# Laying out the inputs by their loads, regrouping on 128 partitions, and two early 128-row blocks in a Fourier-mixing and expert kernel

## The chip, the cores and the metric

The kernel runs on one core of a Trainium2 chip. The core has TensorE (PE, matrix products; its weight loads are shown as PEld), VectorE (DVE), ScalarE (ACT), GpSimd (POOL) and SyncE (SP), which run their own instruction streams and wait for each other through semaphores, and 16 DMA engines that move data between the on-chip memory SBUF and the device memory. SP, ACT and POOL issue DMAs. The metric is the time of one execution on the device, in microseconds; less is better.

## The reference, cut to what matters

Two layers follow each other. The first takes the real part of a two-dimensional Fourier transform of each batch, the second sends each row to one of eight experts, chosen by the largest gate value.

```python
x: (8, 2496, 256)                       # 8 batches, 2496 rows, 256 columns
X = np.fft.fft(np.fft.fft(x, axis=1), axis=2).real
x = X.reshape(19968, 256)
logits = x @ w_gate                      # (19968, 8)
e = argmax(logits); gate_w = softmax(logits)[e]
h = np.maximum(x @ w1[e], 0.0)           # w1[e]: (256, 1024)
y = gate_w * (h @ w2[e])                 # w2[e]: (1024, 256)
```

The weights of one expert are 2 MB in float32.

## The kernel before

All loops are unrolled in Python, and the order in which the instructions are written is the order in which each engine and each queue runs them (`manual_schedule`). Waits are put in by the framework where data or buffers need them.

*The transform.* The 2496 rows of a batch are taken as 104 x 24: row `24 n + j` lies on partition `n` at place `j`. `first(b)` computes the transform along the 104, in `NQ = 3` chunks `q` of four places `j`. Because the input is real, place `j` is combined with its mirror: `load_x` (L269) loads four near places by SP into `xl`, and gathers the mirrored rows by an indirect DMA of POOL, in reversed order, into `xh`; place 0 comes by its own load, `x0`. `fold` (L286) adds the mirror to the near rows on DVE, with reversed columns, and `fold_d` folds the columns; `half1` (L297) multiplies with the wave constants `w1` on PE, and ACT copies out. Then SP stores the result to the device memory, `Td[b]` (L337), and `load(b + 1, q - 1)` loads the next batch into the freed buffers. In three chunks `first` yields 12 times.

`regroup(b, h)` (L347) reads `Td[b]` back in another order, 120 rows on 120 partitions, in two halves of 6 and 5 groups (`t4`). `second(b)` (L357) does the transform along the 24 (`group`), then along the columns together with the gate (`p3`), in two halves `h` of `HW = 5` tiles of 128; each tile gives 2 x 128 rows, the second being mirrored. After each half `route` (L412) finds each row's expert and its place among the expert's rows, and POOL scatters the rows to the array `Xs` in device memory, ordered by expert: ten indirect DMAs (`put_row`, L212) of 128 rows in each half, twenty a batch. `second` yields after each step: 3 times before the first half, then in each half five times for its tiles, three times in `route` and ten times for the scatters.

*The experts.* The rows are worked on in blocks of one expert. `rounds()` (L131) says how many blocks of which size are certain to be there after each batch: after batch 0 two of 256 rows and four of 128, after batch 1 four of 256, then blocks of 512, and at the end 5 of 512, 7 of 256 and 21 of 128 for the rest. `plan` (L463) computes on DVE, from the counters of the experts, a table of each block's first row and expert, which SP reads into registers. `fetch` (L507) issues on SP the block's rows (`xb`, L512) and the two weight matrices (`w_sb`, L515 and L517). `experts` (L533) turns the rows on PE (`pt`), computes the hidden layer (`ph`, evicted with the maximum by ACT and DVE in turn), the second product (`py`), scales it on ACT and scatters 128 rows at a time to the output with POOL (L586). Weights have three buffers; up to three blocks are fetched ahead. 163 row tiles of 128 are computed for 156 of data, since a block has one expert.

*The order.* At the start come constants, the loads of batch 0 and 12 warm-up matmuls. Then `first(0)`, `regroup(0, ...)`, and `second(0)` with the steps of `first(1)` between. Then `experts` runs through the blocks of all rounds, and with it, in steps spread over 70% of each round's work (`TICKS`), the next batch's `second` and the transform `first` of the one after. `sent` and `taken` (L217) tell the framework which scatters a block's rows do not depend on: those of the following round.

Of the kernel before, what the change touches and what calls it, by code (L numbers as in the profile page):

```python
# [130 lines left out]
def rounds():  # L131

    want = [((256, 2), (128, 4)), ((256, 4),)] + [((512, B),)] * (B - 2)
    plan, used = [], 0

    def full(done, size):
        return max(0, -(-(done - used - E * (size - 1)) // size))

    for b in range(B):
        done = (b + 1) * S
        now = []
        for size, most in want[b]:
            k = min(full(done, size), most)
            if k:
                now.append((size, k, False))
            used += size * k
        if b == B - 1:
            k = full(done, BLK)  # L150
            used += BLK * k
            now.append((BLK, k, False))
            now.append((REST, (NT - used + E * (REST - 1)) // REST, True))
        plan.append(now)
    return plan


def in_order():

    todo = []  # L160
    for b, now in enumerate(rounds()):
        parts = [[(b, size, last, i) for i in range(k)] for size, k, last in now]
        if b == B - 1:
            few, many = parts[-2:]
            n = len(many) // len(few)
            rest = [x for i, y in enumerate(few) for x in [y] + many[n * i:n * (i + 1)]] + many[n * len(few):]
            parts = parts[:-2] + [rest]
        todo += sum(parts, [])
    return todo


TICKS = 44
WARM = 12
MOST = max(k for now in rounds() for _, k, _ in now)


# [15 lines left out]
def kernel(ctx: ExitStack, tc, x, w_gate, w1, w2, out):  # L192
# [28 lines left out]
    def taken(ins, b):  # L221
        ins = getattr(ins, "ins", ins)
        if b + 1 < B:
            tc.declare_no_dep(ins, group=f"xs{b + 1}", reason="a block has rows of its round's batches alone")
        tc.add_to_no_dep_group("taken", ins)
# [10 lines left out]

    ix = cp.tile([NA, B, NQ], I32, name="ix")
    pool.iota(ix[:], [[S // 4, B], [-1, NQ]], base=NB // 4 * NA - 1, channel_multiplier=-(NB // 4))
    pad = cp.tile([128, W], F32, name="pad")
# [23 lines left out]
    waves = const_dram("w1", consts["w1"])  # L263


    xall = x.rearrange("b (p j) d -> (b p) j d", j=NB)
    xrows = x.rearrange("b (n j) d -> (b n) (j d)", j=4)

    def load_x(b, q):  # L269
        xl = xp.tile([NP, 4, D], F32, tag="xl", name="xl", bufs=3)  # L270
        xh = xp.tile([NA, 4, D], F32, tag="xh", name="xh", bufs=3)
        n = NP if b + 1 < B else NA
        nc.sync.dma_start(out=xl[0:n], in_=xall[NA * b:NA * b + n, 4 * q + 1:4 * q + 5])
        pool.indirect_dma_start(  # L274
            out=xh[:].rearrange("p j d -> p (j d)"), out_offset=None, in_=xrows,
            in_offset=bass.IndirectOffsetOnAxis(ap=ix[:, b, q:q + 1], axis=0))
        return xl[0:NA], xh[:]

# [6 lines left out]

    def fold(xl, xh, q):  # L286

        n = 3 if q == NQ - 1 else 4
        a, m = xl, xh
        vec.tensor_tensor(free(a, 1, [D, n], [1, D - 1]), free(a, 1, [D, n], [1, D - 1]),  # L290
                          free(m, 3 * D + D - 1, [-D, n], [-1, D - 1]), op=ALU.add)
        yield
        vec.tensor_tensor(free(a, 0, [D, n]), free(a, 0, [D, n]), free(m, 3 * D, [-D, n]), op=ALU.add)
        fold_d(m, a, 4)
        yield
# [14 lines left out]

    def load(b, q):
        if b < B:
            ahead[b, q] = load_x(b, q)
        if b < B and q == 0:
            n = NP if b + 1 < B else NA
            x0 = xp.tile([NP, D], F32, tag="x0", name="x0")
            nc.sync.dma_start(out=x0[0:n], in_=xall[NA * b:NA * b + n, 0])
            ahead[b, "x0"] = x0[0:NA]

    def first(b):  # L320

        pm0 = xp.tile([NA, D], F32, tag="pm0", name="pm0")
        for q in range(NQ + 1):
            f = iter(())
            if q < NQ:
                xl, xh = ahead.pop((b, q))
                f = fold(xl, xh, q)
            next(f, None)
# [6 lines left out]
            if q:  # L335
                half1(b, q - 1, 1, pm, pm0, t1)
                nc.sync.dma_start(out=Td[b][:, 4 * (q - 1) * D:4 * q * D], in_=t1[:].rearrange("p j d -> p (j d)"))  # L337
                load(b + 1, q - 1)
            next(f, None)
            if q == 1:  # L340
                fold_d(pm0[:], ahead.pop((b, "x0")), 1)
            pm = xh
            yield
# [3 lines left out]
    def regroup(b, h):  # L347
        t4 = sp.tile([GP, HALF, D], F32, tag="t4", name="t4")
        n = min(HALF, NG - h * HALF)
        nc.sync.dma_start(  # L350
            out=t4[:, 0:n], in_=bass.AP(Td[b].tensor, Td[b].offset + h * HALF * GP * D,
                                        [[D, GP], [GP * D, n], [1, D]]))
        ahead[b, "t4", h] = t4
# [3 lines left out]
    def second(b):  # L357
# [3 lines left out]
        def turn_last(h):  # L361
# [4 lines left out]
            pr = pm_.tile([GP, HALF], F32, tag="m", name="pr")  # L366
            mm(pr[:, 0:n], con["rot"][:], t4[:, 0:n, H])
            act.copy(t4[:, 0:n, H], pr[:, 0:n])

        def group(g):  # L370
            i, n = g % HALF, LAST if g == NG - 1 else GP
            p2 = pm_.tile([128, 2, n], F32, tag="m", name="p2")
            for c in range(2):
                mm(p2[:, c], t4[:, i, c * H:(c + 1) * H], con["m2"][:, c, 0:n])
            act.copy(zz[:, :, g * GP:g * GP + n], p2[:])  # L375
# [36 lines left out]
    def route(b, h, rows, lg):  # L412
# [40 lines left out]
        for s in range(NSL):  # L453
            sent(put_row(Xs, pi[:, s:s + 1], rows[:, s], E * CAP - 1, "xs"), b)
            yield
# [50 lines left out]

    def fetch(b, size, tab, i):  # L507
        n = size // 128
        row = nc.sync.value_load(tab[:, 0, i:i + 1], min_val=0, max_val=ROWS - size)
        ev = nc.sync.value_load(tab[:, 1, i:i + 1], min_val=0, max_val=E - 1)  # L510
        xb = bp.tile([128, BIG // 128, W], F32, tag="xb", name="xb", bufs=3)
        taken(nc.sync.dma_start(out=xb[:, 0:n].rearrange("p t c -> p (t c)"),  # L512
                                in_=Xs[ds(row, size)].rearrange("(p t) c -> p (t c)", t=n)), b)
        w1_sb = bp.tile([128, 2, F], F32, tag="w1", name="w1_sb", bufs=3)
        nc.sync.dma_start(out=w1_sb[:], in_=w1[ds(ev, 1)].rearrange("o (c p) f -> p (o c) f", p=128))  # L515
        w2_sb = bp.tile([128, FC, D], F32, tag="w2", name="w2_sb", bufs=3)
        nc.sync.dma_start(out=w2_sb[:], in_=w2[ds(ev, 1)].rearrange("o (c p) d -> p (o c) d", p=128))  # L517
        return xb, w1_sb, w2_sb

# [13 lines left out]
    def experts(todo):  # L533
# [5 lines left out]
        def fetch_some(k, most=3):  # L539

            while k + len(got) < len(todo) and len(got) < most and todo[k + len(got)][:3] in tabs:
                b, size, last, at = todo[k + len(got)]
                got.append(fetch(b, size, tabs[b, size, last], at))

        for k, (b, size, last, at) in enumerate(todo):
            n, m = size // 128, BIG // size
            if not k:
                while todo[0][:3] not in tabs:
                    yield 0
                fetch_some(0)  # L550
                for _ in range(9):
                    yield 0
# [38 lines left out]
    def pads(b):  # L591
# [3 lines left out]
        for e in range(E):  # L595
            sent(put_row(Xs, ti[:, e:e + 1], pad[:], ROWS - 1, "xs"), b)
            yield
# [10 lines left out]
    def close(b):  # L608

        for size, k, last in rounds()[b]:  # L610
            yield from plan(b, size, k, last)

# [20 lines left out]
    load(0, 0)  # L633
    act.dma_start(out=con["w1"][:, 4:], in_=waves[:, 4:])
    for _ in range(WARM):
        pw = psy.tile([128, D], F32, tag="y", name="py")
        mm(pw[:], ones[:], bc(ones[:], 1, 2))
    load(0, 1)
    load(0, 2)
    act.dma_start(out=con["rt"][:], in_=const_dram("rt", consts["rt"]))  # L640
    act.dma_start(out=wg[:], in_=w_gate.rearrange("(c p) e -> p c e", p=128))
    nc.sync.dma_start(out=table[:], in_=const_dram("table", packed))
    nc.sync.dma_start(out=bt[:], in_=const_dram("blocks", cv))
    sent(unordered(nc.sync.dma_start(
        out=Xs[E * CAP:].rearrange("(k p) w -> p k w", k=BLK // 128), in_=bc(pad[:], 1, BLK // 128)), "xs"), 0)
    warm = cp.tile([1, 1], F32, name="warm")
# [5 lines left out]
    for _ in first(0):  # L652
        pass
    regroup(0, 0)
    regroup(0, 1)
    vec.tensor_copy(tri[:], con["tri"][:])
    for c in range(2):
# [7 lines left out]
        else:  # L665
            vec.tensor_copy(con["rd"][:, c, to + E:to + 2 * E], pg[:])
    early = ahead_of(1)
    for _ in range(7):
        next(early)
    for k, _ in enumerate(second(0)):  # L670
        if k % 2 == 0:
            next(early, None)
    work = experts(todo)
    for b in range(1, B):

        side, done, due = mixed(b), 0, 0.0
        if b == 1:
            side = woven(close(0), chain(early, side))
        total = 16 * sum(k * size for size, k, _ in rounds()[b - 1]) / BIG
        while done < total:  # L680
# [15 lines left out]


# [18 lines left out]
```

## Time and profile before

The median of 17 executions is 1412.75 us (1408.42 to 1416.7). The profiled execution took 1411.51 us, its span is 1409.7.

| engine | busy us | share of the span | instructions |
|---|---|---|---|
| PE | 1337.8 | 95% | 6186 |
| PEld | 1016.8 | 72% | 6186 |
| DVE | 382.5 | 27% | 1206 |
| POOL | 350.0 | 25% | 360 |
| ACT | 283.2 | 20% | 656 |

In 1409.7 us the DMA engines move 248.81 MB, 176 GB/s. All matmuls but a few are in float32. In the tables below a row names line, engine, operation and tiles as out<-in; `w_sb` stands for both weight tiles, `s`, `p` and `t` for the tiles of the two transform stages, `xT` for the turned rows. A busy time of PE is that of a pipeline and does not say at which clock it ran; the granted clock stands beside it as a share of full speed. "issue" is time in which an engine waited for nothing that the profile shows, "another core or an unknown queue" a wait whose releaser has no record.

### The profile page before, as it was taken

How to read it: one execution, taken by the hardware profiler on the slowest of the kernel's cores; microseconds unless marked ns; L12 is line 12 of the kernel's file. 1: busy time of each engine (PE TensorE's matmuls, PEld its weight loads, DVE VectorE, ACT ScalarE, POOL GpSimd, SP SyncE). 2: the span in 40 equal slices, each digit the busy share in tenths (PEclk: the TensorE clock that was granted, in tenths of full speed). 3: DMA queues.
4: the chain of work that ended last, by engine and by line, in shares of the span. 5: the costliest groups of instructions: out<-in, count | busy, mean ns of one | idle time of the engine just before them, and what ended most of it. 6: DMA issues, size and time to landing. Idle time of an engine off the chain costs nothing.

```text
span 1409.7 us, 17245 instructions
## 1 busy us (share of the span) xinstructions
PE 1337.8 (95%) x6186; PEld 1016.8 (72%) x6186; DVE 382.5 (27%) x1206; ACT 283.2 (20%) x656; POOL 350.0 (25%) x360
## 2 busy tenths in 40 slices
PE   4667898999999999999999999999999999999998
PEld 3556787776677667777677667776667679999997
DVE  3553243333341223332142221233211111111111
ACT  1322132132132111321132211221111111111111
POOL 1343314333214311324113311323311111111111
PEclk9758999999999999999999999999999999999999
DMA  8858877744645442562434442334422348888883
GB/s 233 221 195 262 264 233 236 258 128 121 242 128 176 141 168 94 182 189 100 166 101 138 141 167 94 113 112 143 167 105 97 92 140 272 273 266 267 267 270 99
DMA packets 134517, 248.81 MB, mean 176 GB/s; under 512 B 11245, under 2 KB 93839, under 8 KB 134432
## 3 DMA queue, kind: packets, MB, share of 16 engines
q1 hardware_dynamic: 114438, 194.38, 43.1%
q0 software_dynamic: 19344, 52.37, 10.8%
q10 hardware_dynamic: 650, 0.97, 0.3%
q8 instruction: 49, 0.80, 0.2%
q14 instruction: 36, 0.29, 0.1%
HBM read 194.28 MB, written 54.83 MB: 177 GB/s over the span
## 4 chain that ended last, share of the span: by engine, by line
PE 57%; issue 30%; POOL 6%; DMA 3%; another core or an unknown queue 1%; ACT 1%; DVE 1%; POOLq 0%; SPq 0%; ACTq 0%; DVEq 0%
PE py L197 23%; PE ph L197 23%; PE p L197 6%; POOL out_dram L212 4%; PE s L197 3%; PE pt L528 2%; POOL Xs L212 1%; DMA xh<-in_x_dram,ix 1%; DMA t<-Td 1%; DMA Td<-t 1%; DMA w_sb<-in_moe_w_dram 0%; PE rk L197 0%; POOLq L212 0%; DMA xb<-Xs 0%
## 5 line engine op out<-in xcount | busy, mean ns | idle before, releaser
L197 PE MATMUL ph<-xT,w_sb 128*128 128x512 f32 (+2 forms) x2112 | 589.0, 433 | 4.3 <-ACT hT L572 2.4
L197 PE MATMUL py<-w_sb,hT 128*128 128x256 f32 x2608 | 584.3, 380 | 6.2 <-issue 6.0
L197 PEld LDWEIGHTS py<-w_sb,hT 128*128 128x128 f32 x2608 | 489.4, 191 | 69.7 <-issue 7.0
L197 PEld LDWEIGHTS ph<-xT,w_sb 128*128 128x128 f32 x2112 | 341.8, 192 | 200.0 <-issue 177.1
L212 POOL DMA_INDIRECT out_dram<-y,ro x163 | 158.8, 975 | 849.8 <-ACT y L585 822.0
L570 DVE TENSOR_SCALAR hT<-ph 128x512 f32<-128x512 f32 x163 | 112.7, 692 | 704.9 <-issue 361.6
L585 ACT ACTIVATE y<-py,xb 128x256 f32<-128x256 f32 x163 | 77.1, 473 | 621.0 <-PE py L197 554.0
L212 POOL DMA_INDIRECT Xs<-rows,pi x160 | 158.4, 990 | 126.7 <-issue 78.7
L572 ACT ACTIVATE hT<-ph 128x512 f32<-128x512 f32 x163 | 97.3, 597 | 318.7 <-PE ph L197 297.7
L529 DVE TENSOR_SCALAR xT<-pt,table 128x512 f32<-128x512 f32 (+1 forms) x94 | 63.4, 674 | 64.5 <-PE pt L528 62.9
L197 PE MATMUL s<-xh,w 104*112 104x256 f32 (+2 forms) x208 | 61.9, 423 | 18.6 <-DVE xh L284 16.3
L197 PEld LDWEIGHTS p<-table,t 120*128 120x128 f32 x352 | 56.5, 210 | 28.1 <-issue 13.4
L404 DVE COPY lg<-p 128x16 f32<-128x16 f32 x80 | 14.0, 175 | 209.4 <-ACT zs L401 142.9
L197 PE MATMUL p<-table,zz 128*128 128x145 f32 (+1 forms) x320 | 59.6, 313 | 11.4 <-issue 5.4
L197 PE MATMUL p<-table,t 120*128 120x120 f32 (+1 forms) x352 | 59.5, 296 | 9.6 <-ACT hT L572 4.5
L197 PEld LDWEIGHTS s<-xh,w 104*112 104x112 f32 x208 | 39.6, 204 | 31.7 <-DVE xh L284 14.6
L197 PEld LDWEIGHTS p<-table,zz 128*128 128x128 f32 x320 | 48.3, 205 | 15.7 <-issue 8.2
L528 PEld LDWEIGHTS pt<-table,xb 128*128 128x128 f32 x326 | 40.7, 142 | 16.8 <-issue 11.6
L528 PE MATMUL pt<-table,xb 128*128 128x128 f32 x326 | 51.8, 275 | 0.9 <-DMA xb<-Xs 0.9
L406 DVE SCALAR_TENSOR_TENSOR rows<-p,zs 128x129 f32<-128x129 f32 x160 | 48.4, 344 | 1.6 <-issue 0.4
L274 POOL DMA_INDIRECT xh<-in_x_dram,ix x24 | 24.6, 1024 | 76.3 <-PE s L197 48.9
L375 ACT COPY zz<-p 128x240 f32<-128x240 f32 (+1 forms) x88 | 31.0, 352 | 52.2 <-PE p L197 37.0
(84 smaller groups left out, 333.2 us busy)
## 6 DMA issues: line engine op xcount, KB each, us to landing
w_sb<-in_moe_w_dram SPq DMA_DIRECT2D x132, 1024.0 KB
xb<-Xs SPq DMA_DIRECT2D x28, 516.0 KB
Td<-t SPq DMA_DIRECT2D x24, 448.0 KB
xl<-in_x_dram SPq DMA_DIRECT2D x21, 448.0 KB
t<-Td SPq DMA_DIRECT2D x8, 720.0 KB
t<-Td SPq DMA_DIRECT2D x8, 600.0 KB
xb<-Xs SPq DMA_DIRECT2D x13, 258.0 KB
xb<-Xs SPq DMA_DIRECT2D x25, 129.0 KB
```

The source lines that it names most:

```text
L197: nc.tensor.matmul(o, lhsT=lhsT, rhs=rhs, start=start, stop=stop, **kw)
L212: return unordered(pool.indirect_dma_start(out=dst, out_offset=bass.IndirectOffsetOnAxis(ap=idx, axis=0), in_=rows, in_offset=None, bounds ...
L274: pool.indirect_dma_start(out=xh[:].rearrange("p j d -> p (j d)"), out_offset=None, in_=xrows, in_offset=bass.IndirectOffsetOnAxis(ap=ix[: ...
L375: act.copy(zz[:, :, g * GP:g * GP + n], p2[:])
L404: vec.tensor_copy(lg[:, k:k + 2], p3[:, NY:NY + 2 * E].rearrange("p (m e) -> p m e", m=2))
L406: vec.scalar_tensor_tensor(rows[:, k + m, 0:NY], p3[:, 0:NY], zs[:, 0:1], zs[:, 1:], op0=ALU.add, op1=op)
L528: nc.tensor.transpose(pt[:, c, t], xb[:, 2 * h + t, c * 128:(c + 1) * 128], ident[:])
L529: vec.tensor_scalar(xT[:, :, 256 * h:256 * h + 128 * n], pt[:].rearrange("p c t k -> p c (t k)"), con["alt"][:], None, op0=ALU.mult)
L570: vec.tensor_scalar(o, ph[:], 0.0, None, op0=ALU.max)
L572: act.activation(o, ph[:], ACTF.Relu)
L585: act.activation(y[:, i], py[:], ACTF.Copy, scale=xb[:, i, D + 1:D + 2])
```

## The change

The inputs are laid out anew before the launch, in `laid`: `x` becomes one array in which the 104 partitions' eight places of a load (four near ones and their mirrors, already reversed; place 0 fills a gap of the third) follow each other, 8 KB a partition; the weights become 8 KB a partition in the order of their tiles. So a chunk is one plain load by SP; the gathers of POOL, the index list `ix` and the load of place 0 are gone. `regroup` reads 128 partitions, of which 120 are used. The stores `Td` of batches 0 and 1 are issued by ACT. The loads of batch 1 come after `first(0)`, two ahead of the regroup and one behind it; those of batch 2 are issued together, after the regroup of batch 1.

There is a new first round: two blocks of 128 rows that are certain to be there after the first half of batch 0 is routed; the round after batch 0 has one block of 256 less. The tables for it are computed at steps 11 to 15 of `second(0)` (`AFTER = 10`), the weights of its first block, the regroup of batch 1, the first block's rows and the loads of batch 2 are issued at step 20, in that order, and the steps of `first(1)` go to the places in `FILL`. `fetch` is split in weights and rows. The blocks' independence now covers two following rounds.

```diff
-    want = [((256, 2), (128, 4)), ((256, 4),)] + [((512, B),)] * (B - 2)
+    want = [((128, 2),), ((256, 1), (128, 4)), ((256, 4),)] + [((512, B),)] * (B - 2)
-    for b in range(B):
-        done = (b + 1) * S
+    for b in range(B + 1):
+        done = b * S if b else 2 * 128 * HW - NB
...
-WARM = 12
+WARM = 16
+FILL = (-1,-1,-1,3,5,7,11,11,11,12,13,14)
+ZERO = 3
+AFTER = 5 + HW
...
-    def load_x(b, q):
...
+    def load(b, q):
+        if b < B:
+            xq = xp.tile([NP, 8, D], F32, tag="xq", name="xq", bufs=3)
+            row = (b * NQ + q) * NA
+            nc.sync.dma_start(out=xq[:].rearrange("p j d -> p (j d)"), in_=x[row:row + NP])
+            ahead[b, q] = xq[0:NA]
...
-    def fold(xl, xh, q):
...
+    def fold(xq, q, pm0):
+        a, m = xq[:, 0:4], xq[:, 4:8]
+        n = 4
+        if q == NQ - 1:
+            n = 3
+            fold_d(pm0, m[:, 3], 1)
+        vec.tensor_tensor(a[:, 0:n], a[:, 0:n], m[:, 0:n], op=ALU.add)
+        yield
         fold_d(m, a, 4)
...
-                nc.sync.dma_start(out=Td[b][:, 4 * (q - 1) * D:4 * q * D], in_=t1[:].rearrange("p j d -> p (j d)"))
-                load(b + 1, q - 1)
+                (nc.sync if b > 1 else act).dma_start(out=Td[b][:, 4 * (q - 1) * D:4 * q * D], in_=t1[:].rearrange("p j d -> p (j d)"))
+                if b > 1:
+                    load(b + 1, q - 1)
...
-        t4 = sp.tile([GP, HALF, D], F32, tag="t4", name="t4")
+        t4 = sp.tile([128, HALF, D], F32, tag="t4", name="t4")
...
-            sent(put_row(Xs, pi[:, s:s + 1], rows[:, s], E * CAP - 1, "xs"), b)
+            sent(put_row(Xs, pi[:, s:s + 1], rows[:, s], E * CAP - 1, "xs"), b + 1 if b or h else 0)
...
     def fetch(b, size, tab, i):
...
+        nc.sync.dma_start(out=w1_sb[:], in_=w1[ds(ev, 1)].rearrange("o p c f -> p (o c) f"))
...
+    def fetch_rows(b, size, tab, i):
...
             if not k:
                 while todo[0][:3] not in tabs:
                     yield 0
+                w = fetch(b, size, tabs[b, size, last], at)
+                yield 0
+                got.append((fetch_rows(b, size, tabs[b, size, last], at), *w))
+                yield 0
                 fetch_some(0)
-                for _ in range(9):
+                for _ in range(ZERO):
                     yield 0
...
     load(0, 0)
-    act.dma_start(out=con["w1"][:, 4:], in_=waves[:, 4:])
+    load(0, 1)
+    nc.sync.dma_start(out=con["w1"][:, 4:], in_=waves[:, 4:])
+    load(0, 2)
+    nc.sync.dma_start(out=table[:], in_=const_dram("table", packed))
+    nc.sync.dma_start(out=con["rt"][:], in_=const_dram("rt", consts["rt"]))
+    nc.sync.dma_start(out=wg[:], in_=w_gate)
...
     for _ in first(0):
         pass
+    load(1, 0)
+    load(1, 1)
     regroup(0, 0)
     regroup(0, 1)
+    load(1, 2)
...
-    early = ahead_of(1)
-    for _ in range(7):
-        next(early)
+    early = first(1)
+    work = experts(todo)
+    for _ in range(FILL.count(-1)):
+        next(early, None)
+    first_blocks = plan(0, *rounds()[0][0])
     for k, _ in enumerate(second(0)):
-        if k % 2 == 0:
+        for _ in range(FILL.count(k)):
             next(early, None)
-    work = experts(todo)
+        if k > AFTER:
+            next(first_blocks, None)
+        if k == AFTER + 4:
+            next(work)
+        if k == AFTER + 2 * HW:
+            for _ in early:
+                pass
+            next(work)
+            regroup(1, 0)
+            regroup(1, 1)
+            next(work)
+            for q in range(NQ):
+                load(2, q)
...
+def laid(x, moe_w_gate, moe_w1, moe_w2):
+    n1, i = np.arange(NA)[:, None], np.arange(4)[None]
+    back = -np.arange(D) % D
+    thirds = []
+    for q in range(NQ):
+        s = NB * n1 + 4 * q + 1 + i
+        far = x[:, -s % S][..., back]
+        if q == NQ - 1:
+            far[:, :, 3] = x[:, ::NB]
+        thirds.append(np.concatenate([x[:, s], far], 2))
+    xs = np.stack(thirds, 1).reshape(-1, 8 * D)
...
```

## The prediction

> **What bounds the kernel now.** I read the engine table first, then the tables by stage, the chain of waits and the DMA table. By stage (times in us; busy time and instructions of PE, PEld, DVE, ACT, POOL; granted clock, DMA share, GB/s):
>
> ```profile
> 0.00:43.00 43.00, 18.46 (x58) 12.19 (x58) 17.12 (x45) 6.17 (x10) 7.83 (x12) 0.86 0.87 226
> 43.00:97.00 54.00, 36.45 (x188) 30.35 (x188) 29.46 (x131) 18.14 (x56) 24.65 (x23) 0.66 0.65 192
> 97.00:195.00 98.00, 83.82 (x468) 74.82 (x469) 29.21 (x105) 18.29 (x45) 29.34 (x30) 0.88 0.89 284
> 400.00:1409.00 1009.00, 1004.04 (x4579) 752.55 (x4577) 233.17 (x680) 190.52 (x419) 222.92 (x229) 1.00 0.49 162
> ```
>
> From 400 us on TensorE is busy 1004.04 of 1009 us: nothing there can be won except by giving it less work, and the work stays (163 row tiles of 128). What can be won lies before 400, most of it before 97, when the first expert block starts: until then PE has two transform stages of batch 0 and part of batch 1, small work at a granted clock of 0.66 to 0.86. The chain of waits names what it waits for (start, length, what):
>
> ```profile
> 3.23 15.24 DMA xh<-in_x_dram,ix
> 29.10 7.56 DMA Td<-t
> 36.68 6.32 DMA t<-Td
> 71.03 3.40 another core or an unknown queue
> 87.31 2.34 DMA Xs<-rows,pi
> 90.56 6.45 DMA w_sb<-in_moe_w_dram
> 97.14 3.75 PE ph L197 x8
> 102.72 1.75 PE ph L197 x8
> 122.42 3.01 another core or an unknown queue
> 125.81 3.81 another core or an unknown queue
> 154.80 6.04 issue
> 220.52 8.57 another core or an unknown queue
> 321.84 2.25 issue
> ```
>
> In order: gathered inputs, the store and reload of the transposed batch 0, then (between 60.85 and 88.28, twenty lines of one kind) the scatters of batch 0, and only then the expert weights. The first group of eight hidden-layer matmuls takes 3.75 us, the second 1.75: the first ran on a slow clock. Six pieces with no named releaser sum to 27.1 us. The scatters, from the timeline of POOL, first and last:
>
> ```profile
> 60.85 1.02 POOL L212 DMA_INDIRECT Xs<-rows,pi  x1 [2.79 <-DVE rows L406]
> 87.31 0.97 POOL L212 DMA_INDIRECT Xs<-rows,pi  x1 [0.30 <-issue]
> ```
>
> Each takes 1.0 plus 0.3 us; twenty take 27.4. Last, two DMA rates: the first 45 us, and the best weight loading (270 to 275 us):
>
> ```profile
> DMA packets 4732, 10.26 MB, mean 228 GB/s; under 512 B 805, under 2 KB 2668, under 8 KB 4732
> DMA packets 976, 1.95 MB, mean 391 GB/s; under 512 B 47, under 2 KB 654, under 8 KB 975
> ```
>
> **The change part by part.**
>
> *Inputs.* Now the fold waits for gathers that share the engines with everything issued at the start: the first fold starts at 14.67, the third load's at 21.51, and the last store of batch 0 issues at 29.10, 7.59 after that. The change makes one queue of it in order of need. Up to and with the third load there are 3 x 917 KB of inputs, 186 and 513 KB of wave constants: 3.45 MB. At 228 GB/s that is 15.1 us, at 391 it is 8.8; the first packets move at 1.6 and I give 1.5 for the last to be seen. I take 300 GB/s, between the ends because the rows are now 8 KB in sequence, like the weights, but the first 45 us are the nearest in place: 11.5 + 3.1 = 14.6 (ends 11.9 and 18.2). The three folds before it take 2.76 each (1.22, 0.69, 0.68, 0.17 in the timeline) and do not bind. With the fold of column 0 now ahead of the third add (0.7) the last store issues at 14.6 + 0.7 + 7.6 = 22.9 (20.2 to 26.5).
>
> *Store and regroup.* The store took 7.56 behind 0.9 MB of next-batch loads. It goes to ACT's queue; by 22.9 the issued bytes are 3.45 + 0.77 (tables) + 1.83 (two loads of batch 1, put ahead of the regroup) + 1.38 (stores) = 7.43 MB, 24.8 us at 300 GB/s, so it lands at 28 (ends: 3 us at the fast rate, 7.56 as before). The regroup took 6.32; now 786 KB over 128 partitions at the 235 GB/s of 40 to 45 us, 3.3 + 2 = 5.3 (4.5 to 6.3). Batch 0 can go on at 33.3 instead of 43.0; ends 27.7 and 40.4. *A rule against this:* the Trainium skill (DMA: Bandwidth & Descriptors, "Issuing engines are not separate DMA queues") says that issuing from another engine saves issue time alone, since all queues share the same DMA engines. By it the store would take 7.56 again and the end would be 2.5 us later, inside my slow end; the row cannot tell, as it has one queue only.
>
> *Issue cost.* Six stores on ACT cost 0.3 to 0.6 us of its queue each (its four issues at the start take 0.61, 0.31, 0.38, 0.75); three lie among batch 0's copies, at most 1.5 us on the chain, kept below. Twenty-four gathers of 1.02 + 0.3 us leave POOL; it is 25% busy, and the scatters of batch 0 have none between them, so I take 0. One add instead of two saves DVE 0.16 x 24, hidden: DVE is 27% busy. Four more warm matmuls (0.2 us each) end before the first input. Weights in 8 KB rows: in 145 to 150 us, when 1 KB rows of w2 moved, 278 GB/s; best 391. Where PE is full this is worth 0; in 97 to 195 at most 1 us a block; I take 0.
>
> *Batch 0's second stage.* From its first matmul (43.13) to the first scatter (60.85) are 17.7 us, with 5.1 us of batch 1's matmuls between. Now two of their halves are left there (2 x 0.86 to 1.7): 16 us with ACT's issues. First scatter at 49.5, ten at 62.5, twenty at 76, landed 2.34 later: 64.8 and 78.3, against 89.65 now.
>
> *The two early blocks.* Their rows are fetched at 65. SP has been past the weights of block 0 by then (2.1 MB, no longer after the rows, which saves the 6.45 of the chain), but the two regroups of batch 1 (1.41 MB, 6 us at 235 GB/s) stand ahead in its queue, and they wait for batch 1's stores and for batch 0's last group; three loads of batch 2 stand behind. Rows land near 72. A 128-row block takes 7.25 us at full clock (spacing of the last blocks, 1382.40 to 1389.65), up to twice that on a slow one: 73 to 84. Block 1's weights come last of what is issued from 50 on: 2.1 + 0.9 (stores) + 1.4 + 0.1 + 2.75 + 2.2 + 2.6 (twenty scatters of 132 KB) = 12.1 MB. At 340 GB/s (317 in 90 to 130 us, 363 in 120 to 125) 36 us: 86. Block 1 runs 86 to 94, and the next block of 256 rows, whose rows were there at 78.3 and whose 2.4 MB need 7 us more, starts at 94, not at 97.1 as the first block of 256 does now. *A rule against it:* the Trainium skill (TensorE: Matmul & The Clock Gate, "Why this matters for your kernels") says an idle gap beyond some 3 us puts the array back to half clock. The 3.75 against 1.75 us agree; by it block 0 costs 14.5 instead of 7.25, which my 73 to 84 has room for since block 1 waits for its weights anyway.
>
> *Sum.* 97.1 - 94 = 3.1 earlier, two row tiles of 7.15 already done = 14.3, the cold first group no longer at the head of the long run = 2.0: 19.4. One 256-row block becomes two of 128: 2 x 7.25 - 14.3 = +0.2 and 2 MB more weights, early. The stage 97 to 195 did 8 tiles (57) and 15 of transform in 98 us: 26 lost, taken as unchanged, since two blocks' weights leave it and the rest follows sooner. The profiled execution took 1411.51, 1.24 below the median, inside the spread of 1408.42 to 1416.7: 1411.5 - 19.4 + 0.2 = 1392.
>
> **Rivals.**
>
> *Late transfers.* At the 284 GB/s of 97 to 195 the 12.1 MB last 43 us: block 1 at 93 to 101, the next at 102; with the slow start (40.4) at 107. Then 97.1 - 102 + 14.3 + 2 = 11.4, or about 5: 1400 to 1407, call it 1404. For it: the DMA share is 0.87 to 0.89 in both stages already. Against: 52 to 90 us moves only 161 GB/s now, and that is where the new bytes go.
>
> *More than that.* At the fast ends batch 0 goes on at 27.7 and 12.1 MB take 31 us: the 256-row block at 85, 9 more, 1383. If half of the 27.1 us without a releaser goes with the gathers, 1370; between them 1376. For it: gathers issue at 122.12, 214.65, 223.67 and 319.00, beside four of the stalls. Against: 71 and 154 us have none.
>
> *Slower.* The stalls without a releaser come while scatters and large loads run together (DMA share 0.89 in 125.4 to 129.6 us, 1.07 in 223.3 to 229). The change puts 9 MB of loads beside batch 0's scatters, where today the DMA share is 0.65. Three more of the longest kind, 8.57 each, before 195 us cost 25.7: 1418. It decides from 22 us on.
>
> *It does not do what it says.* If rows of block 0 wait behind the regroups until block 1's weights are there, two blocks run after 86 in one go, and only 7 us fewer are gained: this falls in the late case.
>
> **How the numbers follow.** As forecast 0.5 (1392, own range 1384 to 1400), late 0.2, more 0.21, slower 0.09. About 0.2% (2.8 us) can be told from no change. The range 1373 to 1407 leaves out the slower case and the tails of late and more. Of the slower case 0.01, and of the late one 0.02, end within 0.2% of today: faster 0.89, same 0.03, slower 0.08.
>
> **What would show it.** The last store of batch 0 at 20 to 26 and the first `pr` matmul at 28 to 40; first scatter near 49.5, twentieth near 76 with no gap; first `ph` matmul at 73, two `y` rows by 96, and the first 256-row `ph` at 85 to 102. Wrong, if PE is idle again after 95 for more than the 26 us of today, or if unnamed releasers head the chain between 60 and 100.

## The result, and the profile after

The changed kernel took 1388.98 us (median of 8 runs, 1386.53 to 1393.64) where the kernel before took 1411.96 (46 runs): a ratio of 0.984 with a 95% interval of 0.982 to 0.985, 23 us less. 1392 was predicted. The sum held; as the experiments show, its terms did not, and on another chip the same change is worth 7 us, not 23.

The windows by stage of the changed kernel (time; busy us and instructions of PE, PEld, DVE, ACT, POOL; granted clock, DMA share, GB/s):

```profile
0.00:43.00 43.00, 26.00 (x100) 20.00 (x101) 15.65 (x40) 9.08 (x22) 0.20 (x4) 0.64 0.82 234
43.00:97.00 54.00, 30.55 (x197) 26.93 (x197) 29.00 (x125) 12.03 (x35) 22.56 (x21) 0.78 0.80 260
97.00:195.00 98.00, 89.03 (x539) 79.85 (x538) 41.94 (x154) 26.91 (x74) 27.22 (x28) 0.97 0.76 280
400.00:1389.00 989.00, 985.51 (x4480) 737.12 (x4479) 226.58 (x650) 183.82 (x399) 212.92 (x219) 1.00 0.46 164
```

After 400 us TensorE is as full as before, with 18.5 us less left to do. Between 43 and 97 it is busy for *less* time than before (30.55 against 36.45 us), although two expert blocks now begin there; weighted by the granted clock it is the same work (23.8 against 24.1 us at full clock). The stage that improved is the next one, 97 to 195: 89.03 us busy instead of 83.82, at a granted clock of 0.97 instead of 0.88.

The chain of waits of the changed kernel (start, length, what):

```profile
0.76 6.81 DMA xq<-in_x_dram
...
14.68 10.09 DMA Td<-t
...
25.96 3.06 DMA Td<-t
...
29.08 4.83 DMA t<-Td
...
71.66 15.65 DMA xb<-Xs
...
150.70 10.80 another core or an unknown queue
...
302.56 2.17 issue
...
336.78 3.60 issue
```

The inputs are there at 7.6 instead of 14.7 us, and the regrouped batch 0 at 33.9 instead of 43.0. But two new pieces stand in the chain. At 14.68 the first store of batch 0 takes 10.09 us, and something waits for it; at 71.66 the rows of block 1 take 15.65 us for 129 KB. The timeline shows both (start, length, engine, line, operation; in brackets the idle time before it and what ended it):

```profile
24.85 1.07 ACT L305 COPY t<-s 112x512 f32<-112x512 f32 x2 [6.24 <-DMA Td<-t]
62.06 0.97 POOL L217 DMA_INDIRECT Xs<-rows,pi  x1 [0.30 <-issue]
71.55 0.97 POOL L217 DMA_INDIRECT Xs<-rows,pi  x1 [8.52 <-issue]
74.17 0.69 PE L519 MATMUL pt<-table,xb 128*128 128x128 f32 x2 [4.75 <-DMA xb<-Xs]
78.50 1.23 DVE L290 TENSOR_TENSOR xq<-xq 104x1024 f32<-104x1024 f32 x1 [6.20 <-DMA xq<-in_x_dram]
80.83 5.40 PE L202 MATMUL ph<-xT,w_sb 128*128 128x128 f32 x32 [5.97 <-DVE ro L558]
87.44 0.41 PE L519 MATMUL pt<-table,xb 128*128 128x128 f32 x2 [1.22 <-DMA xb<-Xs]
```

`t1` has two buffers, so ACT's third pair of copies stands until the first store has landed. Block 0's rows are turned at 74.17, but its first `ph` runs at 80.83: the copy to `xT` stands on DVE behind the first fold of batch 2, which waits 6.20 us for its load. The first block of 256 rows starts at 106.56 (97.14 before).

### The profile page after: what moved, and what is told of

It reads as the page before. It is cut to its first block, busy times and chain, and to the rows that moved or that the text cites. A ratio compares the mean times of both kernels' runs of the same rounds, so it can differ in the third digit from the quotient of the medians.

```text
span 1389.8 us, 17247 instructions
## 1 busy us (share of the span) xinstructions
PE 1328.1 (96%) x6222; PEld 1012.2 (73%) x6222; DVE 385.1 (28%) x1204; ACT 283.0 (20%) x656; POOL 324.8 (23%) x335
## 3 DMA queue, kind: packets, MB, share of 16 engines
q10 hardware_dynamic: 885, 2.94, 0.7%
## 4 chain that ended last, share of the span: by engine, by line
PE 56%; issue 30%; POOL 5%; DMA 4%; DVE 2%; ACT 1%; another core or an unknown queue 1%; POOLq 0%; SPq 0%; ACTq 0%; DVEq 0%
PE py L202 23%; PE ph L202 22%; PE p L202 6%; POOL out_dram L217 4%; PE s L202 3%; PE pt L519 2%; DMA xb<-Xs 1%; DMA Td<-t 1%; POOL Xs L217 1%; DMA Xs<-pad,ti 1%; DMA xq<-in_x_dram 0%; DMA t<-Td 0%; PE rk L202 0%; POOLq L217 0%
## 5 line engine op out<-in xcount | busy, mean ns | idle before, releaser
L202 PE MATMUL ph<-xT,w_sb 128*128 128x128 f32 (+2 forms) x2144 | 589.0, 430 | 9.5 <-DVE ro L558 6.0
L202 PE MATMUL s<-xq,w 104*112 104x256 f32 (+2 forms) x208 | 58.1, 402 | 11.0 <-DVE xq L281 7.8
L202 PE MATMUL p<-table,t 120*128 120x120 f32 (+1 forms) x352 | 56.4, 285 | 2.2 <-issue 1.7
L202 PEld LDWEIGHTS p<-table,zz 128*128 128x128 f32 x320 | 46.8, 199 | 12.5 <-ACT zz L363 7.0
L202 PEld LDWEIGHTS s<-xq,w 104*112 104x112 f32 x208 | 37.6, 195 | 24.2 <-issue 9.6
L305 ACT COPY t<-s 112x512 f32<-112x512 f32 x48 | 27.9, 584 | 50.4 <-PE s L202 37.9
```

Of the source, the lines that this page charges most:

```text
L202: nc.tensor.matmul(o, lhsT=lhsT, rhs=rhs, start=start, stop=stop, **kw)
L305: act.copy(t1[:, 2 * half:2 * half + 2], ps[:])
```

## The experiments

One table first, since most verdicts use it. It gives TensorE time lost: for every step of 2 us the idle time of PE, plus its busy time multiplied by one minus the granted clock, added up from the windows; the step that holds an edge counts to the later column. It is rough. In its first column two profiles of nearly the same program and span, 1374.1 and 1373.3, differ by 6.6 us, the clock of the first 43 us being 0.88 in one and 0.76 in the other, where PE mostly waits for inputs. And the span less the three columns, which is the work that is left and should hardly differ, lies between 1312.1 and 1320.9 us. The first four rows were taken where the kernel before takes 1412 us, the others on chips on which it takes 1385.

| kernel | to 97 | 97 to 195 | 195 to 400 | span |
|---|---|---|---|---|
| before | 54.2 | 22.6 | 14.5 | 1409.7 |
| changed | 54.8 | 12.1 | 9.6 | 1389.8 |
| no early blocks (`e1_no_early`) | 57.5 | 17.0 | 8.6 | 1396.8 |
| gathered inputs (`e2_gather`) | 61.4 | 14.7 | 12.5 | 1402.7 |
| before (`c2_before_again`) | 59.9 | 5.7 | 4.1 | 1381.8 |
| changed (`c1_after_again`) | 47.5 | 6.7 | 2.2 | 1374.1 |
| no early blocks (`c3_no_early`) | 46.1 | 0.6 | 2.5 | 1370.1 |
| gathers from batch 2 on (`e11_gather_late`) | 58.1 | 7.0 | 2.4 | 1382.7 |

**Without the early blocks.** The rounds of blocks are those of before, and with them the nine empty steps that the kernel before takes ahead of its first block (`ZERO`, three in the changed kernel) and the scatters that a block waits for; inputs, weights, regroup and stores are as changed:

```diff
-    want = [((128, 2),), ((256, 1), (128, 4)), ((256, 4),)] + [((512, B),)] * (B - 2)
+    want = [((256, 2), (128, 4)), ((256, 4),)] + [((512, B),)] * (B - 2)
...
-ZERO = 3
+ZERO = 9
...
-        if k == AFTER + 4:
-            next(work)
...
```

> The changed kernel without its two early blocks: the rounds of blocks are those of the kernel before (first block 256 rows, after the whole of batch 0), all else as changed. Theory (two gains that add): the early blocks are worth 2 x 7.15 us of row tiles plus about 2 us of cold start, less some 2 us for their weights' traffic, so 1389 + 14 = 1403, and the first 256-row ph starts at about 88, as soon as the twentieth scatter (84.5) has landed, not at 97.1 as before. Rival 1 (the blocks carry all of the gain, the inputs are hidden anyway): about 1411. Rival 2 (the layout and the order of the inputs carry all of it, the blocks only move work): about 1389 to 1392.

Measured: 1395.03 us, ratio to before 0.988 (0.985 to 0.991). The early blocks are worth 6 us here, not 14; the rest of the change is worth 17. Both rivals fall, and the sizes of the theory too: the first 256-row `ph` came at 94.73, not at 88, since it waited for weights that SP issues behind the rows, and the rows behind the twentieth scatter.

**With gathered inputs**, the early blocks kept:

```diff
-            nc.sync.dma_start(out=xq[:].rearrange("p j d -> p (j d)"), in_=x[row:row + NP])
...
+            nc.sync.dma_start(out=xl[0:n], in_=xall[NA * b:NA * b + n, 4 * q + 1:4 * q + 5])
+            pool.indirect_dma_start(
+                out=xh[:].rearrange("p j d -> p (j d)"), out_offset=None, in_=xrows,
+                in_offset=bass.IndirectOffsetOnAxis(ap=ix[:, b, q:q + 1], axis=0))
...
```

> The changed kernel with x in its old layout, half of it gathered by POOL's queue and column 0 loaded by itself, as before; blocks, weights, stores and order of issue as changed. Theory (two gains that add): the first fold starts at 14 to 15 instead of 7.6 and the last store of batch 0 issues 3 to 5 us later than 25.96, so every later step is 3 to 9 us late: 1393 to 1398. Rival 1 (the early blocks carry all): 1389 to 1391, since their start is set by transfers. Rival 2 (the layout carries all): 1403 or more. If the stalls without a named releaser come from the gathers, they grow from 21 us towards 27 us before 400 us; if not, they stay near 21.

Measured: 1406.64 us, ratio 0.997 (0.995 to 0.999): the laid-out inputs are worth 17.7 us. That is rival 2, above all that my sum gave to them. By the table, 6.6 us more than in the changed kernel are lost up to 97 us and 5.5 after it. The chain of waits shows the start, a second place, and one of its pieces without a named releaser:

```profile
3.23 14.71 DMA xh<-in_x_dram,ix
...
27.64 4.58 DMA Td<-t
...
73.59 12.02 DMA xl<-in_x_dram
...
215.34 8.54 another core or an unknown queue
```

**The weights in their old layout, and the regroup on 120 partitions**, one at a time:

```diff
...
-        nc.sync.dma_start(out=w2_sb[:], in_=w2[ds(ev, 1)].rearrange("o p c d -> p (o c) d"))
+        nc.sync.dma_start(out=w2_sb[:], in_=w2[ds(ev, 1)].rearrange("o (c p) d -> p (o c) d", p=128))
```

```diff
-        t4 = sp.tile([128, HALF, D], F32, tag="t4", name="t4")
+        t4 = sp.tile([GP, HALF, D], F32, tag="t4", name="t4")
```

> The changed kernel with the expert weights in their old layout: w2 in rows of 1 KB, w1 in rows of 4 KB instead of 8 KB. As predicted (rows of weights are worth nothing where PE is full, at most 1 us a block before 195 us): 1389 to 1391. Rival: the queues are busy without a break from 58 to 98 us, so that shorter rows slow the 12 MB there from about 340 to 284 GB/s, 7 us: 1396.

> The changed kernel with the regrouped columns loaded on 120 partitions again. As predicted (5.3 against 6.3 us for the first regroup of batch 0, all others hidden): the first regroup takes 6.3 instead of 4.83 us and the time is 1390. Rival: what the first regroup loses is hidden behind the loads that the early blocks wait for: 1389, no difference that can be measured. Second rival: the regroups of batch 1 stand ahead of the rows of the early blocks in the same queue, so their slower transfer costs again: 1392 to 1393.

Measured: 1392.79 (ratio 0.987, 0.984 to 0.989) and 1392.72 (0.988, 0.985 to 0.990). Against 0.984 (0.982 to 0.985) each part seems worth 3 to 4 us, but the first interval overlaps with that of the changed kernel, and the second touches it: small, and not settled. The weights' time lies between the theory and its rival; the regroup's is the number of its second rival, without a trace of that rival's path. The regroup itself took 6.36 us instead of 4.83.

**Three buffers for `t1`**, so that ACT no longer waits for the store:

```diff
-                t1 = xp.tile([NP, 4, D], F32, tag="t1", name="t1")
+                t1 = xp.tile([NP, 4, D], F32, tag="t1", name="t1", bufs=3)
```

> The changed kernel with three buffers for t1 instead of two, so that the third pair of ACT's copies of batch 0 no longer waits 6.24 us for the first store. Theory (that wait was on the path): the last store issues at about 20 instead of 25.96, the first pr matmul starts at 29 to 31 instead of 34.05, and the time is 1384 to 1386. Rival (the bytes bound this stretch, the DMA share is 0.8 to 0.9 up to 27 us): the store issues earlier but lands when it landed, 1388 to 1390.

This run, the next one (both orders), the doubled scatters and the late gathers were made on another chip, where the kernel before took 1384.68 us. Measured: 1376.61, ratio 0.995 (0.993 to 0.997), the same as that of the changed kernel on a third chip (0.996, below). The wait is gone and nothing came of it. ACT in the timeline of this kernel:

```profile
22.67 0.59 ACT L305 COPY t<-s 112x512 f32<-112x512 f32 x1 [4.96 <-PE s L202]
25.80 0.31 ACTq L326 DMA_DIRECT2D Td<-t  x1
```

ACT now waits for PE, which waits for the fold, which waits for the third load; the last store issues at 25.80, as with two buffers (25.96). The rival's cause held, that the transfers bound this stretch; the store does not even issue earlier, as the rival still allowed.

**The order of the queue and of DVE.** First both at once:

```diff
-        if k == AFTER + 4:
+        if k == AFTER + 5:
...
-ZERO = 3
+ZERO = 1
```

> The changed kernel with the first step of the blocks taken one place later in batch 0's second stage, when the table is ready, so that the rows of block 0 stand ahead of the regroups of batch 1 in SP's queue, and rows and weights of block 1 ahead of batch 2's loads; and one empty step instead of three, so that block 0's xT copy stands ahead of the first fold of batch 2 on DVE. Theory (the order of the queue and of DVE held the early blocks back): first ph at 73 to 76 instead of 80.83, both blocks over by 93 instead of 102, time 1383 to 1386. Rival 1 (the transfers between 58 and 98 us bound, the engines are busy there whatever the order): first ph earlier, but the blocks of 256 rows start at 106 as now, 1388 to 1390. Rival 2 (batch 2's loads and batch 1's regroups come later and are missed): 1392 or more.

Measured: 1395.88 us, ratio 1.009 (1.007 to 1.011), 18 us *slower* than the changed kernel on such a chip. The first `ph` did come at 73.58. To part the two edits, the second alone, with no empty step:

```diff
-ZERO = 3
+ZERO = 0
```

> The changed kernel with no empty step between the fetch of block 1 and block 0's transposes (instead of three): block 0's xT copy stands ahead of the first fold of batch 2 on DVE, the order of SP's queue is nearly as it was. Theory (DVE's order cost 5 us there and PE can use them): first ph at about 75 instead of 80.8, block 0 over before block 1's rows land (87), 2 to 4 us faster than the changed kernel. Rival (block 1's rows and weights, which land at 87 and later, set what follows): first ph earlier, the first 256-row ph at 106 as before, no difference. Second rival (what the experiment with both orders showed): batch 2's first fold comes later and block 1's copy waits behind it, 2 to 6 us slower.

Measured, on the chip of the changed kernel's control below: 1393.26 us, ratio 1.007 (1.005 to 1.008), 16 us slower, with the first `ph` at 76.08. The loss lies elsewhere (timeline of this kernel, PE and SP's queue):

```profile
121.19 0.37 SPq L507 DMA_DIRECT2D xb<-Xs  x1
128.60 0.69 PE L519 MATMUL pt<-table,xb 128*128 128x128 f32 x2 [10.59 <-DMA xb<-Xs]
```

In the changed kernel on such a chip the same line reads:

```profile
107.40 0.36 SPq L507 DMA_DIRECT2D xb<-Xs  x1
```

Each empty step of the blocks' generator lets the planning of the next rounds and the transform go one step on. With three fewer the table of the next 128-row blocks (its last write on DVE) is ready at 106.2 instead of 100.3; the fetch then stands in SP's queue behind two stores of batch 2 (109.26 and 118.66), each waiting for ACT's copies, and is issued 13.8 us late. Rival 2 of the first and the second rival of the second had named a loss, with another mechanism. PE waits 10.59 us for these rows; how the 16 us add up beyond that was not traced.

**Doubled scatters** for batches 1 and 2, the second copy to a buffer nothing reads:

```diff
             sent(put_row(Xs, pi[:, s:s + 1], rows[:, s], E * CAP - 1, "xs"), b + 1 if b or h else 0)
+            if b in (1, 2):
+                put_row(Xd, pi[:, s:s + 1], rows[:, s], E * CAP - 1, "xd")
```

> The changed kernel with every row scatter of batches 1 and 2 (40 of them) followed by a second one of the same rows to a buffer that nothing reads. The result and all that waits for it stay; a burst of ten scatters of 1.27 us becomes one of twenty, 12.7 us longer. Theory (signals between the engines come late while a burst of scatters runs, and the stalls without a named releaser end with the burst): the stalls that now end at 158 to 162 and at 241 end with the longer bursts, up to 12 us later each, and 1398 to 1412 comes out, with ACT and DVE idle on an unknown releaser. Rival 1 (the stalls come from loads that share the engines): scatters add 5 MB, 1 to 3 us: 1390 to 1392. Rival 2 (rows arrive late for the blocks): the same loss as the theory, but as named waits of PE for xb.

Measured: 1416.02 us, ratio 1.023 (1.021 to 1.025), 38 us more than the changed kernel there. Rival 2 held: PE waits, by name, at two places, 34.4 us together, and more is lost than the 9 to 23 us above 1389 that it shared with the theory.

```profile
177.93 1.09 PE L522 MATMUL pt<-table,xb 128*128 128x128 f32 x4 [17.58 <-DMA xb<-Xs]
270.82 1.11 PE L522 MATMUL pt<-table,xb 128*128 128x128 f32 x4 [16.85 <-DMA xb<-Xs]
```

The scatters of a batch are no spare time of POOL: the rows of the next round wait for the last of them. The theory could not show itself, because on this chip there was no stall to lengthen.

**Gathers for batches 2 to 7 only**, batches 0 and 1 laid out. The late batches take back their whole old path: the gathers, loads of half the size, a load of column 0 and a second add in the fold.

```diff
+        if 2 <= b < B:
...
+            nc.sync.dma_start(out=xq[0:n, 0:4], in_=xall[NA * b:NA * b + n, 4 * q + 1:4 * q + 5])
+            pool.indirect_dma_start(
+                out=xq[0:NA, 4:8].rearrange("p j d -> p (j d)"), out_offset=None, in_=xrows,
+                in_offset=bass.IndirectOffsetOnAxis(ap=ix[:, b, q:q + 1], axis=0))
...
```

> The changed kernel with batches 0 and 1 loaded in the new layout, and batches 2 to 7 in the old one, with a gather of half of each load in POOL's queue (18 gathers). It tells where the 17.6 us of the gathered inputs go. Theory (about half at the start, half where gathers stand among scatters and folds later): 1396 to 1399. Rival 1 (all of it is the late start of batch 0): 1389 to 1391. Rival 2 (all of it is later, the start is hidden): 1404 to 1407.

Measured: 1384.77 us, ratio 1.001 (1.000 to 1.002): 7 us more than the changed kernel, all that the change gains on such a chip. The expected ranges had been set from the 1389 us of the first chip; as a difference the 7 us are the theory's 7 to 10. The first of these gathers stand in POOL's queue between the tenth and the eleventh scatter of batch 0, ahead of the rows of block 0, which SP issues at 70.23 (68.38 in the changed kernel on such a chip) and which PE gets at 82.72 (73.56 there):

```profile
62.62 0.97 POOL L217 DMA_INDIRECT Xs<-rows,pi  x1 [0.30 <-DMA Xs<-rows,pi]
63.89 1.00 POOL L280 DMA_INDIRECT xq<-in_x_dram,ix  x1 [0.30 <-issue]
65.20 0.99 POOL L280 DMA_INDIRECT xq<-in_x_dram,ix  x1 [0.30 <-issue]
66.50 0.98 POOL L280 DMA_INDIRECT xq<-in_x_dram,ix  x1 [0.31 <-issue]
82.72 0.69 PE L548 MATMUL pt<-table,xb 128*128 128x128 f32 x2 [19.52 <-DMA xb<-Xs]
```

**Controls.** The kernel before took 1412 us in the first four experiments and 1385 in those that followed, so the two kernels and the first experiment were run again.

> The changed kernel itself, as a control. The kernel before took 1412 us in the first four experiments and 1384.7 in the next four, which ran on another chip; there no stall of 5 to 14 us without a named releaser is in any of the four chains, while all profiles taken before have them. Theory (the stalls belong to a chip, not to the gathers or the blocks): where the kernel before takes 1412, the changed one takes 1389 again, ratio 0.984; where it takes 1385, the changed one takes about 1376, ratio 0.994, since the lost TensorE time before 400 us was 61 instead of 76 us in the nearest variant. Rival (the change gains the same on any chip): ratio 0.984 on either, 1362 on the fast one.

> The kernel before itself, for a profile on the chip at hand; the profile that the prediction read was of a chip where it takes 1412. Where it takes 1385: theory (the stalls belong to the chip): no piece of the chain before 400 us without a named releaser above 3 us, and lost TensorE time before 400 us of about 65 us instead of 91. Rival (the stalls belong to the kernel, and something else makes that chip faster): pieces of 3 to 9 us as in the first profile. Where it takes 1412 again, the pieces are there and nothing is told apart.

> The changed kernel without its early blocks once more, to compare with the changed kernel where that takes 1377.6 and the kernel before 1384.6. Theory (the early blocks are worth 6 us on any chip, as in the first run, 1395.03 against 1388.98): about 1383.6, ratio to the kernel before 0.999. Rival 1 (they are worth the 14 us of my sum where no stall disturbs): about 1391, ratio 1.005. Rival 2 (what they do early is given back whole): 1377 to 1379, ratio 0.995. On a chip where the kernel before takes 1412: 1395 again.

Measured, on two more chips where the kernel before took 1384.61 and 1385.96: the changed kernel 1377.64, ratio 0.996 (0.994 to 0.997); the kernel before 1385.21, ratio 1.000 (0.999 to 1.001); the changed kernel without its early blocks 1370.95, ratio 0.989 (0.988 to 0.991). The theory held in the first two (69.7 us lost before 400, where about 65 was expected). They show that the program alone does not make the stalls; every run at 1412 us was also earlier than every run at 1385, and no chip was run twice, so the chip itself and what else differed at the time are not told apart. In the third all cases fall: there the early blocks do not gain 6 us, they *cost* 6.7 by the medians (0.6% by the ratios, from two chips), and the kernel without them beats both. This price has the nine empty steps in it, and three such steps alone moved the time by 16 us above; early blocks with nine empty steps were not run. On the first chip it is the other way round (0.988 against 0.984, intervals that touch). Why the blocks gain there is not shown; what the trace has is that the kernel without them has larger stalls there, unnamed pieces of 14.25 us (at 140.19) and 7.37 us (at 210.30), where the changed kernel has one of 10.80.

The chain of waits of the kernel before on such a chip, all its pieces from 85 to 400 us above 1.5 us that are not work:

```profile
89.11 2.32 DMA Xs<-rows,pi
...
92.33 7.47 DMA w_sb<-in_moe_w_dram
...
233.82 2.42 DMA Xs<-rows,pi
...
236.44 3.98 DMA xb<-Xs
...
333.24 4.24 DMA xb<-Xs
```

The pieces without a releaser that the prediction added up to 27.1 us, 3.01, 3.81, 6.04, 8.57 and 2.25 from 122 us on, are gone, with not a line of the kernel changed. In each of the six profiles with the kernel before at 1412 us (before, changed, the first four experiments) the chain between 120 and 400 us has a piece of 8 to 15 us put down to an unknown queue; in the eight other profiles no piece without a releaser exceeds 1.2 us there.

Without these stalls the windows of 97 to 195 us read, for before, changed, and changed without early blocks:

```profile
97.00:195.00 98.00, 95.34 (x576) 85.58 (x575) 40.56 (x146) 25.81 (x68) 32.52 (x33) 0.97 0.93 310
```

```profile
97.00:195.00 98.00, 93.03 (x575) 83.32 (x574) 46.10 (x170) 29.26 (x78) 30.68 (x32) 0.98 0.79 288
```

```profile
97.00:195.00 98.00, 97.36 (x594) 87.57 (x594) 40.97 (x147) 27.16 (x68) 35.04 (x36) 1.00 0.86 300
```

So there the stage is nearly full even before the change. All of the change but the blocks is worth 15.0 us in the medians, most of it ahead of 97 us (59.9 to 46.1 us lost), some after it (9.8 to 3.1; together the two come out above the 15.0, the table being rough). The first 256-row `ph` without early blocks starts at 91.00, with them at 105.44, after two row tiles, and by 105 us both kernels have lost the same (46.3 and 47.7 us): the early blocks put no work ahead, they trade places with it. Then the kernel with them loses 6 us more up to 165, 2.94 of them where PE waits for rows of the third round:

```profile
159.39 0.63 PE L519 MATMUL pt<-table,xb 128*128 128x128 f32 x4 [2.94 <-DMA xb<-Xs]
```

Without early blocks no wait of PE above 1.5 us is left between 100 and 345 us.

## Why the prediction was right, and where it was not

*Inputs, store and regroup*: last store at 22.9 (20.2 to 26.5), measured 25.96; regroup 5.3, measured 4.83; first `pr` at 33.3, measured 34.05 (43.13 before). Right within its ends. The third load, taken at 14.6 (11.9 to 18.2), let its fold start at 17.49: the 300 GB/s leaned on rows of 8 KB "like the weights", but in the window of the 391 GB/s 654 of 976 packets are under 2 KB, and the slow end was nearer. The step left out that `t1` has two buffers; taking that wait away showed it was covered by the third load.

*The rule of the Trainium skill* (DMA: Bandwidth & Descriptors, "Issuing engines are not separate DMA queues"): the first store on ACT's queue took 10.09 us beside the loads (DMA share 1.02 from 14 to 25 us), the last one, with less beside it (0.69 from 26 to 29), 3.06; it was 7.56 on SP's (0.99 from 29 to 36.7). Another queue by itself spared no transfer time; less under way did. So the rows of this case side with the rule, though not with the 7.56 that the prediction drew from it for the last store: that price was of a store beside more loads than were under way by then.

*Batch 0's second stage*: first scatter 49.5, measured 49.95; the tenth 62.5, measured 62.06. "Twentieth at 76 with no gap" failed: 8.52 us lie between the tenth and the eleventh (3.27 us on the other kind of chip), the twentieth came at 84.48.

*The early blocks* failed in place and in price. Forecast: rows at 72, first `ph` at 73, two `y` rows by 96, the next block at 94. Measured: 74.17, 80.83, the second `y` at 102.19, 106.56. The terms were 3.1 + 14.3 + 2.0 by 97 us; by 97 us the table shows nothing gained (54.2 and 54.8), by 105 us 3.3, within what it is good to. The step that failed is "two row tiles done = 14.3": it counted the tiles as extra, while PE, with the same work at full clock from 43 to 97 (23.8 and 24.1 us), did less of the transform in the same time (99 matmuls of its second stage, `p`, had started by 97 against 124 before). Removing the blocks showed 6.1 us on one kind of chip and minus 6.7 on the other. With the next block at 106.56 this is the schedule of the rival of late transfers (102, or 107 with a slow start), which gave 1400 to 1407.

*"The stage 97 to 195 ... 26 lost, taken as unchanged"* failed the other way: 22.6 to 12.1 us lost by the table, and 14.5 to 9.6 between 195 and 400. These 15 us are most of the 19.9 by which the two spans differ; the table does not place the rest. On the chips without the stalls the change gains nothing in these stages (9.8 and 8.9 us lost), so the 15 go with the stalls without a releaser, some of which I had put into a rival ("more than that", half of 27.1 gone with the gathers). It is not traced piece by piece: the unnamed pieces above 2 us in the chain after 120 us shrank by 7.1 us only, from 23.7 to 10.80 + 2.17 + 3.60. So the predicted time came out by two errors of opposite sign, and that is luck.

*The weights*: 0 taken, up to 4 measured, unsettled. *Issue cost*: the gathers were taken at 0 because POOL is 25% busy. That was wrong. The old path of the late batches alone, with its 18 gathers, costs the whole 7 us on the chips without stalls; what the trace shows of it is that the first three gathers, issued at 63.89 to 67.5, put their 1.3 MB ahead of block 0's 129 KB. The half loads, the loads of column 0 and the second add were not parted from the gathers. *The slower rival* did not come: the longest stall grew, from 8.57 to 10.80 us, but there are fewer.

What stays open: why ACT and DVE wait on one kind of chip. What the trace has: in the changed kernel the 32 `ph` matmuls are recorded from 150.67 to 154.4, and ACT takes its half only as the last scatter of POOL's burst starts, DVE 2 us after that scatter has ended.

```profile
150.67 3.73 PE L202 MATMUL ph<-xT,w_sb 128*128 128x128 f32 x32
158.49 0.97 POOL L217 DMA_INDIRECT Xs<-rows,pi  x1 [0.30 <-issue]
158.57 0.60 ACT L570 ACTIVATE hT<-ph 128x512 f32<-128x512 f32 x1 [7.22 <-remote]
161.55 0.69 DVE L568 TENSOR_SCALAR hT<-ph 128x512 f32<-128x512 f32 x1 [10.85 <-remote]
```

PE's signals for the two halves stand in the trace at 158.50 and 161.45, 4 and 7 us after the last of the matmuls. In each of the six profiles taken where the kernel before takes 1412 us about a quarter of the signals of landed transfers have no record (the changed kernel's holds 7336, on the other chip 9630), so a piece without a releaser there can be a wait whose signal was not recorded. Whether signals are late there by themselves, or because of what records them, no run here tells; it was not tried to stretch the bursts on that chip.

## What to carry to other kernels

An early start is worth what the engine that bounds the end has *more* done at a later moment, not the length of the pieces moved: add up its idle and slow-clock time to the same moment in both kernels. An instruction on an engine that is 25% busy is not free when it, or the transfer that it starts, stands in order ahead of one that others wait for. A stall without a named releaser is not known to be the kernel's until it has been seen on another chip.

## What the runs showed that I had not expected

The kernel before took 1412 us on one chip, and as long in the result's own runs, and 1384.61 to 1385.96 us on three other chips. The same edit was worth 1.6% in the first case and 0.4% on one of the others; the early blocks, with the empty steps that go with them, even change sign. Three empty generator steps, with no instruction in them, were worth 16 us, because they set which fetch stands in front of which store in SP's queue.
